# The opening of a fused attention and expert kernel: chunk 0's inverse placed ahead of the weight conversion and alternated with chunk 1's, chunk 2's scans and scores moved to earlier slots

## The chip, the cores and the metric

The kernel runs on one core of a Trainium2 chip. The metric is the device time of one execution in microseconds (us), the median of several runs of the same kernel. One more execution is recorded by the hardware profiler; every row below is from it.

A core has five engines with one instruction queue each, worked off strictly in order: TensorE (PE; its weight loads are shown as PEld), VectorE (DVE), ScalarE (ACT), GpSimd (POOL) and SyncE (SP), which here only issues DMA transfers. They wait for one another through semaphores.

## The reference, cut to what matters

```
# 1. recurrence over t = 0..767 for 4 batches x 8 heads, head size 40; state is 40 x 40
y[:, :, t]  = einsum('bhd,bhde->bhe', r_t, state)
Sa          = einsum('bhde,bhe->bhd', state, a_t)
state       = state * w_t[:, :, None, :] - einsum('bhd,bhe->bhde', Sa, b_t) \
              + einsum('bhd,bhe->bhde', v_t, k_t)
# 2. x = y as 3072 tokens x 320;   x = ((x @ w_a) * (x @ w_b)) @ w_out        (d_ff 1536)
# 3. top-1 of 8 experts: logits = x @ w_gate; e = argmax; g = softmax(logits)[e]
#    out = g * (relu(x @ w1[e]) @ w2[e])
```

The matrices w_a, w_b and w_out arrive as 64-bit floating point numbers and are multiplied as two parts, high and low.

## The kernel before

**Chunks.** The recurrence is cut into 12 chunks of 64 steps. Within a chunk the chain over time becomes matrix products and the inverse of a triangular matrix for each batch and head. What happens for a chunk, with the lines that do it: the decay is scanned on DVE (`scans`, L558 to L563), k and b are scaled by it (`scale_bk`, L601), a is scaled on GpSimd (`scale_a`, L574) and spread into a block matrix `ablk` by ScalarE (`spread_a`, L578). `scores` multiplies the blocks on PE for one batch at a time (L611), ScalarE copies the result to SBUF (L619), GpSimd masks it (L621), and SP sends it to DRAM (`nd`, L628). It comes back as `m` in another layout (L677 or L679). `rows` does the transposes of k and b (L644, L647); `relayout` copies a decay array into a layout `gp` with six DMAs (L660).

**The inverse.** `tinv(c)` inverts the triangles of chunk c on DVE in 31 steps of two instructions each: `tmp = m * xt` (L686), then `xt = xt - tmp` (L692). A step needs the step before it. The widths run from 31 elements up to 136 and down to 16. After the last one the result goes to DRAM and back into the scores' buffer (L703, L707, L708). Then `t21a` transposes it on DVE (L725) and PE multiplies it (L729); the stages of the chunk on PE follow (L800, L806, L840, L855, L871, L895), with output scores copied by ScalarE (L876) and masked by GpSimd (L878).

**Conversion.** Each matrix of 64-bit words is loaded in pieces of 256 columns (`raw`, L972 to L975; a piece of the third kind has two halves). A piece takes four instructions on DVE (L420, L424, L433, L435), some on ScalarE (L422, L430, L432, and L443 for a piece with two halves) and two or three on GpSimd (L438, then L445 or L440). The four DVE instructions are called steps here; pieces are counted from 0. L433 writes a buffer that GpSimd's L445 of two pieces before reads.

**Order.** PE, DVE, ScalarE and GpSimd work in the order in which the program writes their instructions; SP's order follows from it too. `mix(steps, others)` lays two lists into one another evenly. The opening is written out in `phase1`: scans and scores of chunk 0 and 1, the inverses, conversion. Behind it stands a loop over chunks with 24 slots each. Two tables of numbers, `FIRST` for chunk 0 and `STEADY` for the others, say in which slot a piece of work is issued; `dv` and `ot` are lists of DVE and other steps that are due in later slots. In slot i of chunk 0, `conv[i]` conversion steps and `tinv[i]` steps of the next chunk's inverse are issued.

Of the kernel before, what the change touches and what calls it, by code (L numbers as in the profile page):

```python
# [39 lines left out]
def kernel_body(tc, I, out, stage="full", dbg=None):  # L40
    nc = tc.nc
    ctx = ExitStack()
    with ctx:
# [36 lines left out]
        with ExitStack() as moe:  # L80
            with tc.manual_schedule(engines={E.PE, E.DVE, E.Activation, E.Pool}):
                down = None if stage == "up" else MoeDown(tc, I, moe, psA, psM, ident, hT, wo, xs)
                phase1(tc, I, cst, drm, psA, psM, ident, hT, mk_ident, wo, xs, span, tiny, down)
                if stage == "up":
                    return
                experts = Experts(tc, I, moe, psA, psM, ident, xs, out)
                down.run(experts, span, tiny, flag)
# [32 lines left out]
def mix(steps, others):  # L120

    a, b = len(steps), len(others)
    i = j = 0
    while i < a or j < b:
        if j == b or (i < a and (i + 0.5) * b <= (j + 0.5) * a):
            steps[i]()
            i += 1
        else:
            others[j]()
            j += 1  # L130


def phase1(tc, I, cst, drm, psA, psM, ident, hT, mk_ident, wo, xs, span, tiny, down):
# [4 lines left out]
    A = Attention(tc, I, att, mid, cst, drm, psA, ident, dv, ot, span)  # L138
    A.sink, M.pc = M, A.p2

    def run(fs):
        for f in fs:
            f()

    conv = M.weight_steps()
# [6 lines left out]
    sp = A.p2.tile([128, 2 * 256], I32, tag="raw", name="sp0"), A.p2.tile([128, 2 * 256], I32, tag="raw", name="sp1")  # L152
# [32 lines left out]
    tinv = A.tinv(0)  # L185
# [3 lines left out]
    for pr in range(2):  # L189
        A.scale_a(1, pr)  # L190
        A.spread_a(1, pr)
    n0, n1, n2, n3 = FIRST["conv0"]
    run(conv.take(n0))
    for b in range(B):
        A.scores(1, b)
    for b in range(B):
# [2 lines left out]
    uh = [view(M.p2.tile([128, 2, 256], F32, tag="uh", name=f"m1_{h}")) for h in range(2)]  # L199
    xt = M.p2.tile([128, 2, 256], F32, tag="wo", name="xt1", bufs=1)  # L200
    t1 = A.tinv(1, (uh, view(xt)))
    run(conv.take(n1))
    A.relayout(0)
    A.relayout(1)
    mix(tinv, conv.take(n2))
    A.load_w(2)
    for h in range(2):
        A.load_bk(2, h)
    lead = FIRST["lead"]
    mix(t1[:lead], [lambda: A.forward((0, 0))] + conv.take(n3))  # L210
    t1 = t1[lead:]
    over = [A.spans(0, [t[:120, 0:L // 2].bitcast(F32) for t in sp])]
    units, tinv = [], t1
    for c in range(NCH + 1):
# [10 lines left out]
        for i in range(24):  # L225
# [52 lines left out]
            if c2 < NCH:  # L278
                if c == 0:
# [5 lines left out]
                    for k in range(2):  # L285
                        if i == T["over"][k]:
                            if k:
                                sp = [A.p2.tile([128, 2 * 256], I32, tag="raw", name=f"sp{q + 2}") for q in range(2)]
# [55 lines left out]
            if 2 <= c < 10 and i == T["fill"]:  # L344
                k = nz * (c - 2)
# [5 lines left out]
            tinv = tinv[n:]  # L351
            if i == T["inverse"] and c2 < NCH:
                assert not tinv
                tinv = A.tinv(c2)
# [9 lines left out]
    if not down:  # L364
# [19 lines left out]
FIRST = {  # L384
    "order": [
        [("t21a", 0)], [("t21b", 0), ("t21a", 1)],
        [("pu", 0, 0), ("t21b", 1), ("px", 0, 1)],
        [("stage2p", 0, 1)], [("pu", 0, 1)],
        [("stage2v", 0, 1), ("stage2p", 2, 3)], [], [("stage3", 0, 1)], [],
        [], [("stage4", 0, 1)], [("stage2v", 2, 3)], [],  # L390
        [("stage5", 0, 1), ("stage3", 2, 3)], [], [("px", 1, 0)],
        [("stage4", 2, 3)], [], [], [("stage5", 2, 3)], [], [], [], []],
    "conv0": [8, 6, 10, 8], "lead": 16, "early": 13, "extra": [10, 17], "ones": [2, 14],
    "conv": [
# [6 lines left out]
    "load_a": [19, 21], "r00": [2, 3, 4], "r1": [8, 9, 10], "score": [15, 16, 17, 18], "row": [16, 17, 22, 23],  # L401
    "tinv": [4, 4, 4, 4, 4, 4, 4, 4, 4, 4, 4, 2, 0, 0, 0, 0, 0, 0, 0, 0, 0, 0, 0, 0], "relayout": 14, "load_w": 15,
    "span": 18, "scan": [21, 22, 22, 23, 23],
}

# [1428 lines left out]
```

## Time and profile before

| what | value |
|---|---|
| median of 3 runs | 1122.64 us (1122.29 to 1123.97) |
| profiled execution, its time | 1123.74 us |
| profiled execution, its span | 1122.0 us |
| PE busy | 987.2 us, 88% of the span |
| DVE busy | 699.5 us, 62% |
| ACT busy | 592.1 us, 53% |
| POOL busy | 422.8 us, 38% |

The span runs from the first to the last instruction that the profiler saw; the time of that execution lies a little over it. A busy share is a mean over the whole span: it says nothing on which engine the others wait for in a given stretch, for which the rows further down are cut by time.

### The profile page before, as it was taken

Reading aid. Unit: us, or ns where it says so; the run is one execution under the profiler, and the core shown is the slowest. Engines: PE = TensorE matmul, PEld = TensorE weight load, DVE = VectorE, ACT = ScalarE, POOL = GpSimd, SP = SyncE. Lnnn points to the kernel's source line nnn. Section 1 sums busy time; section 2 is a strip of 40 time slices with the busy share of each in tenths; the row PEclk is TensorE's granted clock in tenths of the full one; section 3 lists DMA queues with packets and bytes.
Section 4 is the critical chain, followed back from the end, with each engine's and each line's share of the span. In section 5 each row is a group of like instructions: output and inputs, shape, how many; then the busy total and the mean of one; then the engine's idle time right before and its main releaser. Section 6 shows DMA issues by size and latency. Waiting matters only on the chain.

```text
span 1122.0 us, 27118 instructions
## 1 busy us (share of the span) xinstructions
PE 987.2 (88%) x10402; PEld 948.1 (85%) x10402; DVE 699.5 (62%) x1843; ACT 592.1 (53%) x1373; POOL 422.8 (38%) x469
## 2 busy tenths in 40 slices
PE   4064587999899999999999999999999999999994
PEld 4053587989889899999898999999999898999994
DVE  8889689677787878787866731336667733222230
ACT  5367866666666666666665453333334354444430
POOL 4327645233323323343333113002224466666641
PEclk9656689999999999999999999979999999999997
DMA  8553454476758476675746223825557264444500
GB/s 209 149 159 82 99 135 104 124 144 166 146 153 172 129 168 145 136 157 143 152 130 122 76 75 90 239 68 159 182 177 236 87 220 139 141 146 140 160 17 16
DMA packets 200664, 154.11 MB, mean 137 GB/s; under 512 B 107269, under 2 KB 182630, under 8 KB 200524
## 3 DMA queue, kind: packets, MB, share of 16 engines
q1 hardware_dynamic: 187196, 132.91, 44.8%
q0 software_dynamic: 9808, 15.76, 5.6%
q10 hardware_dynamic: 3520, 3.61, 1.2%
q8 instruction: 84, 1.38, 0.5%
q14 instruction: 56, 0.46, 0.1%
HBM read 103.66 MB, written 44.60 MB: 132 GB/s over the span
## 4 chain that ended last, share of the span: by engine, by line
PE 71%; DVE 10%; DMA 6%; ACT 5%; issue 4%; SPq 2%; POOL 1%; POOLq 0%; DVEq 0%; ACTq 0%
PE pm L1071 23%; PE py L1208 9%; PE u L1497 8%; PE dn L1517 7%; PE s1p L611 4%; PE p L871 3%; PE pp L855 2%; PE py L895 2%; PE px L800 2%; DVE xt L692 1%; PE ta L729 1%; DMA out<-y,ids 1%; DVE tmp L686 1%; PE tb L748 1%; PE px L791 1%
## 5 line engine op out<-in xcount | busy, mean ns | idle before, releaser
L878 POOL TENSOR_SCALAR_AFFINE_SELECT s<-s 64x512 f32<-64x512 f32 x96 | 72.4, 755 | 180.8 <-ACT s L876 176.6
L686 DVE TENSOR_TENSOR tmp<-m,xt 128x126 f32<-128x126 f32 (+22 forms) x372 | 115.1, 310 | 30.5 <-DMA xt<-in_one 19.0
L1083 DVE TENSOR_TENSOR uh<-pm,ua 128x256 f32<-128x256 f32 x144 | 60.4, 419 | 114.5 <-PE pm L1071 67.1
L1071 PE MATMUL pm<-xl,wh 128*128 128x256 f32 x576 | 130.7, 309 | 0.8 <-ACT ua L1074 0.8
L1500 DVE SCALAR_TENSOR_TENSOR hl<-u,hh 128x384 fp32r<-128x384 f32 (+5 forms) x72 | 41.5, 580 | 140.1 <-ACT hh L1499 140.1
L692 DVE TENSOR_TENSOR xt<-xt,tmp 128x126 f32<-128x126 f32 (+22 forms) x372 | 115.3, 310 | 8.6
L1071 PE MATMUL pm<-xh,wl 128*128 128x256 f32 x576 | 117.7, 286 | 0.0
L1071 PE MATMUL pm<-xh,wh 128*128 128x256 f32 x576 | 117.6, 286 | 0.0
L1071 PEld LDWEIGHTS pm<-xl,wh 128*128 128x128 f32 x576 | 90.5, 195 | 3.5 <-ACT ua L1074 1.2
L1208 PE MATMUL py<-wh,hl 128*128 128x328 f32 x288 | 91.3, 317 | 2.0 <-DVE hl L1198 2.0
L1208 PE MATMUL py<-wl,hh 128*128 128x328 f32 x288 | 92.3, 321 | 0.6 <-DVE wl L1179 0.6
L1071 PEld LDWEIGHTS pm<-xh,wh 128*128 128x128 f32 x576 | 91.7, 196 | 0.0
L1071 PEld LDWEIGHTS pm<-xh,wl 128*128 128x128 f32 x576 | 91.4, 195 | 0.0
L1208 PE MATMUL py<-wh,hh 128*128 128x328 f32 x288 | 90.9, 316 | 0.0
L611 PE MATMUL s1p<-ablk,bk 120*128 120x192 f32 (+1 forms) x264 | 53.1, 345 | 41.6 <-ACT ablk L578 30.1
L611 PEld LDWEIGHTS s1p<-ablk,bk 120*128 120x128 f32 x264 | 47.0, 211 | 44.3 <-ACT ablk L578 43.8
L1071 PE MATMUL pm<-xh,w 128*128 128x256 f32 x288 | 82.7, 287 | 0.0
L1071 PE MATMUL pm<-xl,w 128*128 128x256 f32 x288 | 82.6, 287 | 0.0
L1261 POOL DMA_INDIRECT xs<-xr,si x24 | 28.0, 1166 | 137.4 <-DVE acc L1256 89.2
L1074 ACT COPY ua<-pm 128x256 f32<-128x256 f32 x144 | 53.4, 371 | 46.8 <-PE pm L1071 44.3
L1517 PE MATMUL dn<-l,hh 128*128 128x320 f32 (+3 forms) x240 | 74.9, 312 | 0.0
L1517 PE MATMUL dn<-h,hl 128*128 128x320 f32 (+3 forms) x240 | 74.1, 309 | 0.0
(238 smaller groups left out, 2775.4 us busy)
## 6 DMA issues: line engine op xcount, KB each, us to landing
hT<-uh SPq DMA_DIRECT2D x72, 256.0 KB
hf<-hT SPq DMA_DIRECT2D x36, 512.0 KB
r<-in_moe_w SPq DMA_DIRECT2D x8, 1280.0 KB
r<-in_moe_w SPq DMA_DIRECT2D x8, 1024.0 KB
bk<-in_bk SPq DMA_DIRECT2D x22, 360.0 KB
xs<-zt SPq DMA_DIRECT2D x8, 805.0 KB
m<-nd SPq DMA_DIRECT2D x44, 128.0 KB
at<-in_a SPq DMA_DIRECT2D x24, 180.0 KB
```

The source lines that it names most:

```text
L611: nc.tensor.matmul(ps[:2 * C, 3 * g * C:(3 * g + n) * C], self.bk5(c, b, g), self.ablk[b // 2][:, b % 2, g, 0:n, 0:C], start=True, stop=True)
L686: nc.vector.tensor_tensor(box[0], m[2 * s // R][:, s % (R // 2):s % (R // 2) + 1, s + 1:].to_broadcast([128, rows, n]), xt[:, :rows, s:s + ...
L692: nc.vector.tensor_tensor(xt[:, :rows, s + 1:], xt[:, :rows, s + 1:], box[0], op=ALU.subtract)
L871: nc.tensor.matmul(p2[b][:, 3 * g * C:(3 * g + n) * C], self.cur[b]["uv"][:, 128 * g:128 * g + 128], self.rblk[:, b % 2, g, 0:n, 0:C], sta ...
L878: nc.gpsimd.affine_select(out=s2t[q * C:q * C + C], in_=s2t[q * C:q * C + C], pattern=[[0, 8], [1, C]], base=0, channel_multiplier=-1, com ...
L1071: nc.tensor.matmul(p, l, r, start=(i == 0), stop=(i == len(seq) - 1))
L1074: nc.scalar.copy(a, p)
L1083: nc.vector.tensor_tensor(h[:, f % 2], p, a, op=ALU.mult)
L1208: self.nc.tensor.matmul(py, self.pair[i][l][:, k, s], self.W[r][:, first + k, cols], start=(first + k == 0 and n == 0), stop=(first + k == ...
L1497: nc.tensor.matmul(p, l, r, start=(i == 0), stop=(i == len(seq) - 1))
L1500: nc.vector.scalar_tensor_tensor(out=hl, in0=p, scalar=0.0, in1=hh.bitcast(F32), op0=ALU.max, op1=ALU.subtract)
L1517: nc.tensor.matmul(p, l[:, q], r[:, f], start=(f == 0 and i == 0), stop=(f == len(hs) - 1 and i == 2))
```

## The change

It touches the opening and the table for chunk 0. The eight conversion steps that stood ahead of chunk 1's scores, and six behind chunk 1's `rows`, are no longer there; the first 28 instructions of chunk 0's inverse come first on DVE, mixed with 16 conversion steps, and the other 34 are mixed one to one with the first 34 of chunk 1's. Four more of chunk 1's, chunk 0's first stages and four conversion steps follow. The slots' table takes three conversion steps in each of the first twelve slots instead of two, and 24 instructions of chunk 1's inverse in six slots instead of 46 in twelve. Chunk 2's decay limits, scans, scaling, blocks and scores are issued in earlier slots. No instruction is added or taken away; DVE has as many as before.

```diff
-    n0, n1, n2, n3 = FIRST["conv0"]
-    run(conv.take(n0))
     for b in range(B):
         A.scores(1, b)
...
     t1 = A.tinv(1, (uh, view(xt)))
-    run(conv.take(n1))
     A.relayout(0)
     A.relayout(1)
-    mix(tinv, conv.take(n2))
+    n0, n1 = FIRST["conv0"]
+    lead = FIRST["lead"]
+    mix(tinv[:lead], conv.take(n0))
+    k = len(tinv) - lead
+    mix(tinv[lead:], t1[:k])
     A.load_w(2)
     for h in range(2):
         A.load_bk(2, h)
-    lead = FIRST["lead"]
-    mix(t1[:lead], [lambda: A.forward((0, 0))] + conv.take(n3))
-    t1 = t1[lead:]
+    mix(t1[k:k + 4], [lambda: A.forward((0, 0))] + conv.take(n1))
+    t1 = t1[k + 4:]
...
-    "conv0": [8, 6, 10, 8], "lead": 16, "early": 13, "extra": [10, 17], "ones": [2, 14],
+    "conv0": [16, 4], "lead": 28, "early": 13, "extra": [10, 17], "ones": [2, 14],
...
-    "over": [2, 7], "span2": 4, "scan2": 9, "bk": [12, 13], "sa": [12, 13], "sp": [[13, 14, 15], [14, 15, 16]],
+    "over": [2, 7], "span2": 1, "scan2": 3, "bk": [6, 7], "sa": [6, 7], "sp": [[7, 8, 9], [8, 9, 10]],
```

On DVE the order of before has three whole pieces of conversion behind the scaling of chunk 1's k and b. The rows are the third piece's, the start of the fourth, and the start of chunk 0's inverse; `c_f` and `c_s` are a piece's buffers, `raw0_1_0` its words, `m0` and `xt0` belong to chunk 0's inverse.

```order
L420 TENSOR_SCALAR c_f_367<-raw0_1_0_171 128x256
L424 SCALAR_TENSOR_TENSOR c_f_367<-raw0_1_0_171,c_f_367 128x256
L433 TENSOR_SCALAR c_s_368<-c_f_367 128x256
L435 SCALAR_TENSOR_TENSOR c_s_368<-raw0_1_0_171,c_s_368 128x256
L420 TENSOR_SCALAR c_f_382<-raw0_1_1_278 128x256
L424 SCALAR_TENSOR_TENSOR c_f_382<-raw0_1_1_278,c_f_382 128x256
L686 TENSOR_TENSOR tmp0_0_402<-m0_242,xt0_243 128x31
L692 TENSOR_TENSOR xt0_243<-xt0_243,tmp0_0_402 128x31
```

In the new order of DVE the inverse follows the scaling at once, and the fourth piece's first step is row 49, counted from the program's start. The first piece below is from around it, the second from where chunk 0's fifteenth step begins to alternate with chunk 1's first.

```order
L692 TENSOR_TENSOR xt0_243<-xt0_243,tmp0_10_421 128x6x21
L420 TENSOR_SCALAR c_f_429<-raw0_1_1_374 128x256
L686 TENSOR_TENSOR tmp0_11_434<-m0_242,xt0_243 128x120
L692 TENSOR_TENSOR xt0_243<-xt0_243,tmp0_11_434 128x6x20
L424 SCALAR_TENSOR_TENSOR c_f_429<-raw0_1_1_374,c_f_429 128x256
L686 TENSOR_TENSOR tmp0_12_438<-m0_242,xt0_243 128x133
```

```order
L686 TENSOR_TENSOR tmp0_14_448<-m0_242,xt0_243 128x136
L686 TENSOR_TENSOR tmp1_0_450<-m1_0_323,xt1_325 128x31
L692 TENSOR_TENSOR xt0_243<-xt0_243,tmp0_14_448 128x8x17
L692 TENSOR_TENSOR xt1_325<-xt1_325,tmp1_0_450 128x31
L686 TENSOR_TENSOR tmp0_15_454<-m0_242,xt0_243 128x128
L686 TENSOR_TENSOR tmp1_1_456<-m1_0_323,xt1_325 128x30
L692 TENSOR_TENSOR xt0_243<-xt0_243,tmp0_15_454 128x8x16
L692 TENSOR_TENSOR xt1_325<-xt1_325,tmp1_1_456 128x30
```

The fourth piece's first step stood ahead of the inverse; now it stands 34 rows into it, and in the 68 alternating rows there is nothing but the two inverses.

On SP the fourth piece's load stood behind chunk 0's second r and ahead of chunk 1's scores on their way to DRAM.

```order
L588 DMA r0_1_255<-in_r 120x384
L972 DMA raw0_1_1_278<-in_moe_w_b 128x512
L628 DMA nd1_128<-s1_1_0_295 32x8x32 x4
L628 DMA nd1_128<-s1_1_1_312 32x8x32 x4
L680 DMA xt1_351<-in_one 128x512
L677 DMA m1_0_349<-nd1_128 32x512
```

In the new order of SP it stands behind the loads of chunk 1's m and behind both relayouts, whose last rows these are.

```order
L660 DMA gp0_335<-w0_113 64x4x64 x2
L660 DMA gp1_342<-w30_r_124 120x4x64
L660 DMA gp1_342<-w30_r_124 8x4x64
L660 DMA gp1_342<-w30_r_124 112x4x64
L660 DMA gp1_342<-w30_r_124 16x4x64
L660 DMA gp1_342<-w30_r_124 64x4x64 x2
L972 DMA raw0_1_1_374<-in_moe_w_b 128x512
L974 DMA raw0_0_2_400<-in_moe_w_a 64x512
L975 DMA raw0_0_2_400<-in_moe_w_b 64x512
L972 DMA raw256_0_0_426<-in_moe_w_a 128x512
```

The load moved behind eight loads of m and twelve issues of the relayouts.

On GpSimd, behind the masks of chunk 0's first pair of output scores, the new order reads as follows (`s2_0_1` is an output score, `s1_2_0` a score of chunk 2, `at2` chunk 2's a).

```order
L878 AFFINE_SELECT s2_0_1_962<-s2_0_1_962 64x512 x2
L574 TENSOR_TENSOR at2_1_642<-at2_1_642,w2_562 120x384
L438 TENSOR_TENSOR c_f_936<-c_f_936,w30_0_596 64x256
L438 TENSOR_TENSOR c_f_936<-c_f_936,w31_0_597 64x256
L440 TENSOR_TENSOR c_f_936<-c_f_936,c_s_937 128x256
L438 TENSOR_TENSOR c_f_985<-c_f_985,wh00_0_351 128x256
L445 TENSOR_TENSOR wl0_107<-c_f_985,c_s_986 128x256
L621 AFFINE_SELECT s1_2_0_1021<-s1_2_0_1021 64x512 x2
L438 TENSOR_TENSOR c_f_1005<-c_f_1005,wh01_0_376 128x256
L445 TENSOR_TENSOR wl0_107<-c_f_1005,c_s_1006 128x256
```

Before, the first L621 of chunk 2's scores stood further back, behind the masks of the second pair of output scores, the scaling of `at2_1`, a piece with two halves and `xl` (L1050):

```order
L878 AFFINE_SELECT s2_0_3_1106<-s2_0_3_1106 64x512 x2
L574 TENSOR_TENSOR at2_1_654<-at2_1_654,w2_545 120x384
L544 MEMSET d1_91 120x13
L438 TENSOR_TENSOR c_f_1084<-c_f_1084,w30_1_1082 64x256
L438 TENSOR_TENSOR c_f_1084<-c_f_1084,w31_1_1083 64x256
L440 TENSOR_TENSOR c_f_1084<-c_f_1084,c_s_1085 128x256
L1050 TENSOR_TENSOR xl0_1147<-xf0_0_1093,xh0_1146 128x3x128
L621 AFFINE_SELECT s1_2_0_1183<-s1_2_0_1183 64x512
L438 TENSOR_TENSOR c_f_1140<-c_f_1140,wh00_1_1139 128x256
L445 TENSOR_TENSOR wl0_107<-c_f_1140,c_s_1141 128x256
L621 AFFINE_SELECT s1_2_0_1183<-s1_2_0_1183 64x512
L621 AFFINE_SELECT s1_2_1_1251<-s1_2_1_1251 64x512
```

Chunk 2's four masks moved ahead of the second pair's, in between pieces 10 to 13. On ScalarE the blocks of ablk moved as well: the third block for chunk 2's first score stands twelve rows behind L443 of piece 9, and before five rows behind L443 of piece 14.

## Rows read from the trace of the kernel before

**Rows 1.** The page: busy tenths of the span in 40 slices of 28 us.

```profile
PE   4064587999899999999999999999999999999994
DVE  8889689677787878787866731336667733222230
```

**Rows 2.** Windows: stretch, length, busy time and instructions by engine, TensorE clock, DMA.

```profile
31.30:55.60 24.30, 0.00 (x0) 0.00 (x0) 21.15 (x73) 7.09 (x20) 5.86 (x8) 0.55 0.59 156
87.90:111.70 23.80, 9.24 (x97) 8.29 (x97) 21.62 (x38) 16.22 (x45) 19.51 (x23) 0.65 0.37 85
```

**Rows 3.** Timeline of DVE: start, length (both us), engine, line, operation, tiles.

```profile
42.57 0.29 DVE L686 TENSOR_TENSOR tmp<-m,xt 128x126 f32<-128x126 f32 x1
42.90 0.29 DVE L692 TENSOR_TENSOR xt<-xt,tmp 128x126 f32<-128x126 f32 x1
43.10 0.29 DVE L433 TENSOR_SCALAR c_s<-c_f 128x256 int32<-128x256 int32 x1
...
54.98 0.60 DVE L692 TENSOR_TENSOR xt<-xt,tmp 128x16 f32<-128x16 f32 x1
...
55.71 0.19 DVE L692 TENSOR_TENSOR xt<-xt,tmp 128x31 f32<-128x31 f32 x1
55.93 0.19 DVE L686 TENSOR_TENSOR tmp<-m,xt 128x30 f32<-128x30 f32 x1
56.04 0.42 DVE L435 SCALAR_TENSOR_TENSOR c_s<-raw,c_s 128x256 f32<-128x256 uint32 x1
...
62.31 0.89 DVE L725 STREAM_TRANSPOSE t<-s 32x256 f32<-32x256 f32 x2
```

**Rows 4.** Timeline of SP's queue: length is the time of issuing.

```profile
26.07 0.40 SPq L972 DMA_DIRECT2D raw<-in_moe_w_b  x1
...
31.93 3.56 SPq L677 DMA_DIRECT2D m<-nd  x8
...
37.38 5.15 SPq L660 DMA_DIRECT2D gp<-w  x6
42.57 4.46 SPq L660 DMA_DIRECT2D gp<-w_r  x6
```

**Rows 5.** Chain that ended last, cut to the first 260 us: from issue to landing.

```profile
36.11 2.76 DMA raw<-in_moe_w_b
```

**Rows 6.** Timeline of PE; brackets: idle time before, who ended it.

```profile
62.88 0.28 PE L729 MATMUL ta<-t,s 32*32 32x32 f32 x2 [33.07 <-DVE t L725]
...
112.79 2.07 PE L611 MATMUL s1p<-ablk,bk 120*128 120x192 f32 x6 [11.52 <-DVE c_f L420]
```

**Rows 7.** Timeline of ACT.

```profile
87.22 1.06 ACT L876 COPY s<-p 128x512 f32<-128x512 f32 x2
...
109.67 0.83 ACT L443 CAST w<-c_f 64x256 fp32r<-64x256 f32 x2 [1.83 <-POOL c_f L440]
```

**Rows 8.** Timeline of POOL.

```profile
87.86 4.34 POOL L878 TENSOR_SCALAR_AFFINE_SELECT s<-s 64x512 f32<-64x512 f32 x4 [7.41 <-ACT s L876]
...
102.71 3.27 POOL L878 TENSOR_SCALAR_AFFINE_SELECT s<-s 64x512 f32<-64x512 f32 x4
...
107.19 1.65 POOL L438 TENSOR_TENSOR c_f<-c_f,w 64x256 f32<-64x256 f32 x2
...
111.44 1.17 POOL L1050 TENSOR_TENSOR xl<-xf,xh 128x384 fp32r<-128x384 f32 x1 [1.80 <-ACT xh L1049]
...
116.41 0.72 POOL L438 TENSOR_TENSOR c_f<-c_f,wh 128x256 f32<-128x256 f32 x1
...
123.38 0.65 POOL L621 TENSOR_SCALAR_AFFINE_SELECT s<-s 64x512 f32<-64x512 f32 x1
```

**Rows 9.** Timeline of DVE, up to chunk 1's first transposes.

```profile
117.97 0.29 DVE L433 TENSOR_SCALAR c_s<-c_f 128x256 int32<-128x256 int32 x1 [4.75 <-POOL wl L445]
...
123.46 1.41 DVE L433 TENSOR_SCALAR c_s<-c_f 128x256 int32<-128x256 int32 x1 [4.08 <-POOL wl L445]
...
131.11 0.89 DVE L725 STREAM_TRANSPOSE t<-s 32x256 f32<-32x256 f32 x2
```

More of the change, by code (lines that the diff above doesn't have):

```diff
@@ L399 @@
         2, 1, 2, 1, 2, 1, 2, 1, 2, 2, 1, 1],
[1 row of a table removed]
-    "load_a": [19, 21], "r00": [2, 3, 4], "r1": [8, 9, 10], "score": [15, 16, 17, 18], "row": [16, 17, 22, 23],
-    "tinv": [4, 4, 4, 4, 4, 4, 4, 4, 4, 4, 4, 2, 0, 0, 0, 0, 0, 0, 0, 0, 0, 0, 0, 0], "relayout": 14, "load_w": 15,
[1 row of a table added]
+    "load_a": [19, 21], "r00": [2, 3, 4], "r1": [8, 9, 10], "score": [9, 10, 11, 12], "row": [12, 17, 22, 23],
+    "tinv": [4, 4, 4, 4, 4, 4, 0, 0, 0, 0, 0, 0, 0, 0, 0, 0, 0, 0, 0, 0, 0, 0, 0, 0], "relayout": 14, "load_w": 15,
     "span": 18, "scan": [21, 22, 22, 23, 23],
```

2 rows, old and new, of the table FIRST are left out of this document.

## The prediction

> **What bounds the kernel now.** I read the busy tenths first. VectorE (DVE) is at 8 or 9 in most of the first seven slices of 28 us while TensorE (PE) stands between 0 and 7; from the eighth slice on PE stands at 8 or 9 [rows 1]. So the opening belongs to DVE and what feeds it, the rest to PE, and time gained or lost in the opening shifts all that follows. The order says where the change ends: from the 226th row on, 18 rows ahead of chunk 1's transposes (L725), DVE's orders read the same, PE's from chunk 1's first L729. So the forecast is one question: when does DVE begin those transposes? Before it is 131.11 us [rows 9]; a shift there I carry to the end unchanged, since DVE and PE have little idle time behind it [rows 1].
>
> Next the windows and DVE's timeline. From 31.30 to 55.60 DVE works through chunk 0's inverse with ten conversion steps between, 73 rows in 24.30 us, 0.333 us a row, and PE does nothing [rows 2]. Single starts tell what a step costs. A product 126 elements wide starts at 42.57, the subtraction that needs it at 42.90: 0.33. The next instruction, which needs neither, starts 0.20 later [rows 3]. Narrow ones (30 or 31 wide): 0.22 to a dependent one, 0.11 to an independent one [rows 3]. So a step that doesn't need the result just before it starts a third to a half sooner; this is what alternation can give.
>
> Last subtraction 54.98, its end 0.60 later, hence 55.58 [rows 3]; the inverse goes out through SyncE's queue (SP) to DRAM and back, and DVE's transposes start at 62.31 [rows 3], PE's first L729 at 62.88 after 33.07 us of idling [rows 6]. That tail is 62.31 - 55.58 = 6.7 us.
>
> **Part 1: the conversions behind the scores, and a load that moves with them.** No conversion step stands ahead of the inverse any more. This removes a load's early place too: the fourth piece's words (raw0_1_1, L972) were sent at 26.07, ahead of chunk 1's scores' way to DRAM [rows 4]. In the new order of SP they stand behind the 8 loads of chunk 1's m (L677) and behind all 12 issues of the two relayouts (L660). Those cost SP: the m loads end at 31.93 + 3.56 = 35.49; the relayouts take 5.15 + 4.46 = 9.61 [rows 4]. One issue of 0.40 leaves ahead of them [rows 4], two other pieces that stood between no longer do, so the last relayout is issued at 35.49 - 0.40 + 9.61 = 44.7. A load of such words landed 2.76 after its issue [rows 5]: 47.5. (If the scores come up to 2 us earlier, since ScalarE and DVE have no conversion in front of them, 45.5; that is the lower bound.)
>
> DVE needs that piece in its 49th row, the 35th after the inverse starts. Even if the inverse started only at the old 31.3, the 34 rows at 0.333 are done by 42.6. So DVE waits, everything on it queued behind, until about 47.5: a wait of at least 5 us that wasn't there.
>
> **Part 2: alternation.** Behind the wait stand ten rows of mixed steps, at the mean of 0.33 and 0.20: 2.7 us, hence 50.2. Then 68 rows alternate chunk 0's last 34 steps with chunk 1's first 34. Their mean width, counted from the order, is 96; between 0.11 at 30 and 0.20 at 126 that is 0.17 a row, 11.7 us: chunk 0's inverse ends at 61.9. With dependent starts throughout (0.22 and 0.33, so 0.295) it would be 20.1. I take 0.17, since the row of an independent successor is the nearest.
>
> 61.9 - 55.6 = **+6.3 us** for everything that waits for chunk 0's inverse. The work that DVE has then done is about the same as before at 62 (it has 18 of chunk 1's steps more, 15 of the conversion's fewer). With the tail of 6.7 us PE starts at 62.88 + 6.3 = 69.2. In this tail DVE's new order has only 8 rows: little is left to cover the round trip with.
>
> **Part 3: chunk 2's scans and scores earlier.** Their instructions are the same in number; they shift on ScalarE and GpSimd, among them ablk's blocks (L578) and GpSimd's masks (L621). From PE's start, the chain to the first output score copies of chunk 0 (L876) keeps its instructions: 87.22 [rows 7] + 6.3 = 93.5. GpSimd masks them from 94.1 (87.86 before) for 4.34 [rows 8], then, in its order, a scaling of chunk 2's a (0.72 for 256 columns, so about 1.1 for its 384), and two products and a sum for piece 9, which took 2.5 from 107.19 until L443 was let go at 109.67 [rows 7, 8]: 102.0. ScalarE's L443 waits for that sum, as it did before at 109.67 with 1.83 of idling [rows 7]; now the blocks of ablk for chunk 2's first score stand behind it, after 18 instructions at 16.22 / 45 = 0.36 [rows 2] L443's own 0.83, and two DMA issues at 0.40 or somewhat more [rows 4], taken at 1.0: 102.0 + 0.8 + 6.5 + 1.0 = 110.3. So the first score of chunk 2 starts on PE at about 111, against 112.79 before [rows 6]: placed 45 rows earlier, it gains no more than 2 us. PE has nearly the same rows from there to the last of the four scores (6 matmuls of L840 for 6 of L644), so the last mask comes as far behind as before, 123.38 - 112.79 = 10.6 [rows 6, 8]: at 121.6.
>
> What stands behind that last mask on GpSimd changes most. Before: two pieces, 4 instructions of 0.72. Now: the mask's own 0.65, piece 13 (2 x 0.72 = 1.5), the masks of chunk 0's second pair (4.34), piece 14 (2.4), the round over ScalarE to xl (1.80 idle, 1.17 of work), and pieces 15 to 18 (4 x 1.5) [rows 8]. Sum 0.65 + 1.5 + 4.3 + 2.4 + 1.8 + 1.2 + 6.0 = 17.9: GpSimd is through at 121.6 + 17.9 = 139.5. DVE's L433 can't write its buffer before GpSimd has done L445 of two pieces back: twice before it waited for that, 4.75 and 4.08 us [rows 9]. So its last two conversion steps start at 139.5 and take about 1.2 (an estimate between the 2 x 0.29 of an undisturbed L433 and the 2 x 1.41 of a slow one [rows 9]): the transposes stand at 140.7, against 131.11: **+9.6 us**.
>
> The profiled execution took 1123.74; 1123.74 + 9.6 = 1133.3. It lies 1.1 over the median of the runs, so the median to come is 1132.2, said as **1132**. Bounds of this case: the load 2 us sooner and the second pair's masks at their shorter 3.27 [rows 8] give +6.5, i.e. 1129; two waits more of the length of 1.8 on GpSimd's way give 1136.
>
> **A rule weighed against the trace.** The row pair shows 0.33 to a dependent step and 0.20 to an independent one [rows 3]. The Trainium skill, "VectorE: DVE Perf Modes", section "The DRAIN you can't avoid", has the next operation start only when the pipe of eight stages is empty; by that alone alternation would give nothing and the 68 rows would cost 20.1. The same page's section "Two Vector instructions with no wait between them" says that one that isn't held starts earlier, which agrees with the 0.20. The first reading is the third rival.
>
> **The rivals.**
> *Faster.* If chunk 2's scores really come early, GpSimd doesn't wait for them and doesn't hold DVE: the two waits of 4.75 and 4.08 [rows 9] go, 8.8 us, against the 6.3: 1122.6 + 6.3 - 8.8 = 1120; without part 1's wait it would be some 5 better. For it: GpSimd's work from 102.0 to the end of piece 15 is only 18 us (pieces 10 to 13 and 15 at 1.5, four masks at 0.65, the second pair's 4.3, piece 14's 2.4, xl's 1.2), so without waits it is there at 120, just when DVE, 6.3 late, comes to need it. It decides by GpSimd's waiting in that stretch: what it waits there comes off the 8.8, and above 2.5 us in all nothing is won. I find more than that at the first mask alone, which stands only 1.5 us of work behind the sum that releases L443, while ScalarE and PE need some 11 from L443 to that score. 13 in 100.
>
> *Only the delay.* The stretch from the copies to the transposes takes as long as before, 131.11 - 87.22 = 43.9, since what the early scores win on ScalarE they lose on GpSimd: +6.3, so 1129. For it: DVE was idle for 8.8 us there, and can run ahead. 22 in 100.
>
> *Each operation waits for the one before it to drain.* Then 8.4 more in part 2: 1132 + 8.4 = 1140. Against: the 0.20 and the 0.11 [rows 3]. 5 in 100; 2 more for other ways above 1136.
>
> *No change.* DVE's work up to the transposes is the same, and its waits only change their names: the wait for the load takes the place of those for GpSimd, within 2.2 us. For it: 4.75 + 4.08 is not far from 6.3 plus the tail's idling. 10 in 100.
>
> **How the numbers follow.** My forecast, 1129 to 1136 with 1132 the likeliest, has 48 in 100. A measurement tells about 0.2%, 2.2 us, from no change. Faster holds 0.13, same 0.10, slower 0.48 + 0.22 + 0.07 = 0.77. The range from 1121 to 1139 takes in forecast, delay alone and no change, and leaves out most of the faster case and the drained one.
>
> **What would show it.** In the changed kernel's trace: a wait of DVE at L420 for raw from in_moe_w_b, ending near 47; rows of 0.17 in the alternating stretch; PE's first L729 near 69; an L443 on ScalarE that ends a wait for GpSimd near 102; chunk 2's last mask near 122; chunk 1's transposes near 141. I am wrong if DVE's 49th row finds its words there, if GpSimd runs without waits from 100 to 130, or if PE's steady part takes back what the opening lost.

## The result and the profile after

The changed kernel takes 1135.93 us (median of 4 runs, 1134.41 to 1136.44) against 1122.52 for the kernel before, measured with it: ratio 1.0133, interval 1.0115 to 1.0151 (the plain quotient of the two medians is 1.0119, near the interval's lower end). It is slower, by a little over one per cent; the forecast range, 1129 to 1136, just holds the time, 4 us above its likeliest value. The profiled execution took 1136.14 us, its span 1134.3.

The page's busy tenths, to be held against [rows 1]: PE first reaches 9 in the ninth slice and no longer in the eighth, and DVE's second slice falls from 8 to 5.

```profile
PE   4042568899999989999999999999999899999994
DVE  6568489686979778796878651335666842222230
```

SP's queue in the changed kernel (start, time of issuing) answers to [rows 4]. The fourth piece's load goes out at 46.06, behind the relayouts, where before it went out at 26.07; the last line is chunk 0's inverse on its way to DRAM.

```profile
32.62 3.57 SPq L677 DMA_DIRECT2D m<-nd  x8
36.29 4.71 SPq L660 DMA_DIRECT2D gp<-w  x6
41.11 4.91 SPq L660 DMA_DIRECT2D gp<-w_r  x6
46.06 0.61 SPq L972 DMA_DIRECT2D raw<-in_moe_w_b  x1
...
64.50 2.65 SPq L703 DMA_DIRECT2D td<-xt  x4
```

DVE's timeline in the changed kernel answers to [rows 3, 9]. The wait of 11.26 us at L420 is the one forecast; the 7.70 at L558, the first scan step of chunk 2, was not. The rows marked x2 show the alternation: two instructions each, the next row 0.33 later, so some 0.17 an instruction. The last wait for GpSimd ahead of the transposes ends at 139.49; from there DVE works through 9.0 us of rows of its own without waiting.

```profile
37.15 0.78 DVE L692 TENSOR_TENSOR xt<-xt,tmp 128x126 f32<-128x126 f32 x1
49.18 0.29 DVE L420 TENSOR_SCALAR c_f<-raw 128x256 int32<-128x256 int32 x1 [11.26 <-DMA raw<-in_moe_w_b]
...
52.32 0.89 DVE L686 TENSOR_TENSOR tmp<-m,xt 128x136 f32<-128x136 f32 x2
53.15 0.40 DVE L692 TENSOR_TENSOR xt<-xt,tmp 128x136 f32<-128x136 f32 x2
53.48 0.39 DVE L686 TENSOR_TENSOR tmp<-m,xt 128x128 f32<-128x128 f32 x2
...
64.63 0.29 DVE L686 TENSOR_TENSOR tmp<-m,xt 128x126 f32<-128x126 f32 x1
...
69.58 0.90 DVE L725 STREAM_TRANSPOSE t<-s 32x256 f32<-32x256 f32 x2 [2.98 <-DMA s<-td]
...
83.90 0.65 DVE L558 TENSOR_SCALAR w<-w 120x768 f32<-120x768 f32 x1 [7.70 <-ACT junk L537]
...
123.66 0.29 DVE L433 TENSOR_SCALAR c_s<-c_f 128x256 int32<-128x256 int32 x1 [9.20 <-POOL wl L445]
...
139.49 0.29 DVE L433 TENSOR_SCALAR c_s<-c_f 128x256 int32<-128x256 int32 x1 [3.40 <-POOL wl L445]
...
147.36 0.75 DVE L433 TENSOR_SCALAR c_s<-c_f 128x256 int32<-128x256 int32 x1
...
148.48 0.89 DVE L725 STREAM_TRANSPOSE t<-s 32x256 f32<-32x256 f32 x2
```

PE's timeline answers to [rows 6]: the first L729 at 70.16, then a wait of 5.32 at L840 for DVE's rows (L850), which stand behind L558 there, and chunk 2's first score at 114.84 after 18.55 us of idling for its blocks.

```profile
70.16 0.28 PE L729 MATMUL ta<-t,s 32*32 32x32 f32 x2 [40.21 <-DVE t L725]
...
90.69 0.89 PE L840 MATMUL pv<-ident,vn 128*120 128x128 f32 x3 [5.32 <-DVE tp L850]
...
114.84 2.07 PE L611 MATMUL s1p<-ablk,bk 120*128 120x192 f32 x6 [18.55 <-ACT ablk L578]
```

ScalarE, answering to [rows 7]: chunk 2's decay limits (L537), whose last row ends at 83.87, just ahead of DVE's L558, and which stand behind L736, which waited for PE's first L729; the output score copies at 98.72, the first block at 99.80, L443 after 6.06 us of waiting for GpSimd, the third block with the next at 114.19.

```profile
71.62 0.78 ACT L736 ACTIVATE pt<-ta 32x256 f32<-32x256 f32 x2 [4.67 <-PE ta L729]
...
83.68 0.19 ACT L537 ACTIVATION_READ_ACCUMULATOR junk<-w,wlim 120x1 f32 x1
...
98.72 1.06 ACT L876 COPY s<-p 128x512 f32<-128x512 f32 x2
99.80 0.62 ACT L578 ACTIVATE ablk<-at,bd 120x384 f32<-120x384 f32 x1
106.48 0.83 ACT L443 CAST w<-c_f 64x256 fp32r<-64x256 f32 x2 [6.06 <-POOL c_f L440]
...
114.19 1.10 ACT L578 ACTIVATE ablk<-at,bd 120x384 f32<-120x384 f32 x2
```

GpSimd, answering to [rows 8]: three waits for ScalarE between 106 and 122, the last mask of chunk 2 at 126.57, the last L445 ahead of the transposes at 145.11.

```profile
111.48 0.72 POOL L438 TENSOR_TENSOR c_f<-c_f,wh 128x256 f32<-128x256 f32 x1 [5.04 <-ACT wh L432]
...
117.66 0.66 POOL L621 TENSOR_SCALAR_AFFINE_SELECT s<-s 64x512 f32<-64x512 f32 x1 [4.65 <-ACT s L619]
121.48 0.65 POOL L621 TENSOR_SCALAR_AFFINE_SELECT s<-s 64x512 f32<-64x512 f32 x1 [3.16 <-ACT s L619]
...
126.57 0.65 POOL L621 TENSOR_SCALAR_AFFINE_SELECT s<-s 64x512 f32<-64x512 f32 x1
...
145.11 0.72 POOL L445 TENSOR_TENSOR wl<-c_f,c_s 128x256 fp32r<-128x256 f32 x1
```

### The profile page after: what moved, and what is told of

It reads as the page before. It is cut to its first block, busy times and chain, and to the rows that moved or that the text cites. A ratio compares the mean times of both kernels' runs of the same rounds, so it can differ in the third digit from the quotient of the medians.

```text
span 1134.3 us, 27119 instructions
## 1 busy us (share of the span) xinstructions
PE 982.0 (87%) x10402; PEld 943.4 (83%) x10402; DVE 690.7 (61%) x1843; ACT 592.1 (52%) x1373; POOL 422.3 (37%) x469
## 4 chain that ended last, share of the span: by engine, by line
PE 67%; DVE 12%; ACT 6%; DMA 5%; issue 5%; POOL 3%; SPq 1%; ACTq 0%; POOLq 0%; DVEq 0%
PE pm L1071 23%; PE py L1208 9%; PE u L1497 6%; PE dn L1517 6%; PE s1p L611 4%; PE p L871 3%; PE pp L855 2%; PE py L895 2%; DVE xt L692 2%; DMA out<-y,ids 2%; PE px L800 2%; DVE tmp L686 1%; PE ta L729 1%; PE kbp L644 1%; PE tb L748 1%
## 5 line engine op out<-in xcount | busy, mean ns | idle before, releaser
L686 DVE TENSOR_TENSOR tmp<-m,xt 128x126 f32<-128x126 f32 (+22 forms) x372 | 110.1, 300 | 31.1 <-DMA xt<-in_one 17.8
L1208 PE MATMUL py<-wh,hl 128*128 128x328 f32 x288 | 91.1, 316 | 2.0 <-DVE hl L1198 2.0
L1208 PE MATMUL py<-wl,hh 128*128 128x328 f32 x288 | 92.1, 320 | 0.6 <-DVE wl L1179 0.6
L1208 PE MATMUL py<-wh,hh 128*128 128x328 f32 x288 | 90.7, 315 | 0.0
L611 PEld LDWEIGHTS s1p<-ablk,bk 120*128 120x128 f32 x264 | 46.7, 210 | 51.6 <-ACT ablk L578 51.1
L1074 ACT COPY ua<-pm 128x256 f32<-128x256 f32 x144 | 53.5, 371 | 44.5 <-PE pm L1071 42.5
L729 PE MATMUL ta<-t,s 32*32 32x32 f32 x768 | 22.6, 202 | 60.5 <-DVE t L725 56.8
```

Of the source, the lines that this page charges most:

```text
L611: nc.tensor.matmul(ps[:2 * C, 3 * g * C:(3 * g + n) * C], self.bk5(c, b, g), self.ablk[b // 2][:, b % 2, g, 0:n, 0:C], start=True, stop=True)
L686: nc.vector.tensor_tensor(box[0], m[2 * s // R][:, s % (R // 2):s % (R // 2) + 1, s + 1:].to_broadcast([128, rows, n]), xt[:, :rows, s:s + ...
L1074: nc.scalar.copy(a, p)
L1208: self.nc.tensor.matmul(py, self.pair[i][l][:, k, s], self.W[r][:, first + k, cols], start=(first + k == 0 and n == 0), stop=(first + k == ...
```

## The experiments

My theory: the change loses by places in queues, first the load behind the relayouts, then the early scores, whose blocks and masks hold conversion. The rivals: the early scores set the pace whatever the load does; or the order of DVE's work as such (inverse first, conversion pushed back) costs the time. Single executions of the kernel before spread from 1117 to 1128 us beside these runs, so ratios to it are compared. The ratio on record differs from the plain quotient of the medians by up to 0.0015; differences as small as that are not read here. The table puts four marks (starts, us) beside the ratio; the marks come from one execution of each kernel, the ratio from all.

| kernel | ratio (interval) | PE's first L729 | first L876 | chunk 2's first score | chunk 1's first L729 |
|---|---|---|---|---|---|
| before | 1 | 62.88 | 87.22 | 112.79 | 131.68 |
| changed | 1.0133 (1.0115 to 1.0151) | 70.16 | 98.72 | 114.84 | 149.06 |
| early load | 1.0069 (1.0050 to 1.0089) | 59.63 | 91.12 | 107.19 | 141.89 |
| old slots | 1.0095 (1.0073 to 1.0118) | 68.14 | 92.61 | 123.63 | 143.87 |
| old opening, early slots | 1.0008 (0.9992 to 1.0024) | 63.20 | 90.30 | 101.86 | 136.24 |
| early load, old slots | 1.0030 (1.0017 to 1.0043) | 59.16 | 86.11 | 118.06 | 137.67 |
| the same, no alternation | 1.0058 (1.0041 to 1.0075) | 64.62 | 88.94 | 119.97 | 139.59 |
| early load, limits earlier | 1.0025 (1.0011 to 1.0039) | 59.17 | 85.96 | 102.39 | 136.62 |
| conversion beside the inverse | 1.0022 (1.0003 to 1.0041) | 61.53 | 90.00 | 115.16 | 134.38 |
| relayouts behind | 1.0065 (1.0046 to 1.0084) | 58.74 | 87.27 | 103.33 | 138.18 |
| the former, four pieces ahead | 0.9978 (0.9958 to 0.9997) | 62.03 | 85.00 | 110.55 | 131.58 |
| change, queues mended | 1.0012 (0.9995 to 1.0029) | 58.97 | 82.67 | 99.23 | 135.18 |
| the same, blocks ahead of L443 | 0.9973 (0.9958 to 0.9988) | 58.25 | 81.99 | 84.97 | 128.44 |
| before with two mends | 0.9935 (0.9912 to 0.9959) | 61.30 | 84.27 | 103.98 | 124.16 |

("The former" is conversion beside the inverse.) The ratio goes, by and large, with the last column and not with the first: nine kernels start PE's work on chunk 0 earlier than before, and only three of them are faster.

**Early load.**

```diff
-        self.ahead = lambda: [load(j) for j in range(3)]
+        self.ahead = lambda: [load(j) for j in range(4)]
```

> The changed kernel, with the fourth piece's words loaded together with the first three (ahead of chunk 0's scores), all else as changed. Theory A (the load's wait costs what it lasts): the wait of 11.26 us at DVE's L420 is gone, chunk 0's inverse ends near 53 instead of 64.5, PE's first L729 stands near 59 instead of 70.2, and the time falls by 9 to 11 us, to about 1126. Theory B (the early scores set the pace on ScalarE and GpSimd whatever chunk 0's inverse does): the wait goes, PE starts near 59, but chunk 1's transposes come less than 5 us earlier than 148.5 and the time stays above 1131.

The wait at the fourth piece's L420 is gone, chunk 0's inverse goes out at 53.64, PE starts at 59.63, as theory A said; 10.5 us there. The ratio falls from 1.0133 to 1.0069, some 7 us (6 by the medians), less than the 9 to 11 expected. Behind PE's start a new wait for words has come in, for the seventh piece, and the wait at L558 is still there:

```profile
68.48 0.29 DVE L420 TENSOR_SCALAR c_f<-raw 128x256 int32<-128x256 int32 x1 [4.96 <-DMA raw<-in_moe_w_a]
...
76.30 0.65 DVE L558 TENSOR_SCALAR w<-w 120x768 f32<-120x768 f32 x1 [5.66 <-ACT junk L537]
```

**Old slots for chunk 2, the changed opening.**

```diff
-    "over": [2, 7], "span2": 1, "scan2": 3, "bk": [6, 7], "sa": [6, 7], "sp": [[7, 8, 9], [8, 9, 10]],
+    "over": [2, 7], "span2": 4, "scan2": 9, "bk": [12, 13], "sa": [12, 13], "sp": [[13, 14, 15], [14, 15, 16]],
...
-    "load_a": [19, 21], "r00": [2, 3, 4], "r1": [8, 9, 10], "score": [9, 10, 11, 12], "row": [12, 17, 22, 23],
+    "load_a": [19, 21], "r00": [2, 3, 4], "r1": [8, 9, 10], "score": [15, 16, 17, 18], "row": [16, 17, 22, 23],
```

> The changed opening, with chunk 2's limits, scans, scaling, blocks and scores back in the slots of before. Theory A (part delay, part early scores): PE's first L729 stays at 70 and the wait of 11 us at L420 stays; the wait of 7.70 at DVE's L558 and the longer road from chunk 0's output score copies to chunk 1's transposes (49.8 us, 43.9 before) go back to before's; chunk 1's transposes near 138 to 139, time about 1129. Theory B (early scores cost nothing, the delay is all): time within 2 us of the changed kernel, 1134 or more.

Between the two: 1.0095, where A said 1129 (1.006); its interval touches the changed kernel's. The wait at L420 stays (9.40 us), the wait of 7.70 at L558 is gone, but the other sign of A failed: the road from the first L876 to chunk 1's first L729 (last column less second) stays long, 51.3 us against 50.3 in the changed kernel and 44.5 before. So the early slots alone don't make this road longer than before.

**Old opening, early slots** (edit on the kernel before).

```diff
-    "over": [2, 7], "span2": 4, "scan2": 9, "bk": [12, 13], "sa": [12, 13], "sp": [[13, 14, 15], [14, 15, 16]],
+    "over": [2, 7], "span2": 1, "scan2": 3, "bk": [6, 7], "sa": [6, 7], "sp": [[7, 8, 9], [8, 9, 10]],
...
-    "load_a": [19, 21], "r00": [2, 3, 4], "r1": [8, 9, 10], "score": [15, 16, 17, 18], "row": [16, 17, 22, 23],
+    "load_a": [19, 21], "r00": [2, 3, 4], "r1": [8, 9, 10], "score": [9, 10, 11, 12], "row": [12, 17, 22, 23],
```

> The opening of before with chunk 2's limits, scans, scaling, blocks and scores in the changed kernel's early slots; conversion and inverse steps per slot as before. Theory A: no wait at L420, PE's first L729 near 63, but L558 waits for ScalarE's limits and GpSimd's masks wait for the scores: chunk 1's transposes 6 to 10 us later than 131, time 1128 to 1132. Theory B (early scores are a gain that the late inverse hid): chunk 1's transposes earlier than 131 and a time below 1120.

Neither: no difference (1.0008). L558 waits 5.89 us and chunk 1's first L729 comes 4.6 us late, yet nearly all of it comes back by the end. The road from the copies is 45.9 us, 1.5 more than before. Chunk 2's first score comes at 101.86, 11 us earlier than before, and DVE's waits for GpSimd don't go by it: 3.04, 5.42, 1.42 and 3.41 ahead of the transposes. So the early slots alone explain little of the loss, and win nothing either.

**Early load and old slots.**

> The changed opening with the fourth piece loaded early and chunk 2's work in the slots of before: what is left of the change is the inverse ahead of conversion and the alternation. Theory A: chunk 0's inverse ends near 53, two to three us before the 55.6 of the kernel before, PE's first L729 near 60, and chunk 1's transposes come as much earlier: 1119 to 1120.5. Theory B (work is only moved about, DVE has the same to do until chunk 1's transposes): 1122 to 1124.

Theory A failed here, and the time, 1125.29, lies a little above B's range as well. PE starts at 59.16, 3.7 us earlier than in the kernel before, and chunk 1's transposes still come 6 us late. DVE again waits for words at L420, and longer than before for GpSimd's pieces:

```profile
68.44 0.29 DVE L420 TENSOR_SCALAR c_f<-raw 128x256 int32<-128x256 int32 x1 [5.38 <-DMA raw<-in_moe_w_a]
...
74.03 0.46 DVE L420 TENSOR_SCALAR c_f<-raw 128x256 int32<-128x256 int32 x1 [3.16 <-DMA raw<-in_moe_w_b]
...
93.82 0.29 DVE L433 TENSOR_SCALAR c_s<-c_f 128x256 int32<-128x256 int32 x1 [3.65 <-POOL c_f L440]
```

The words are now behind the round trip of the earlier inverse: on SP the seventh piece's load is issued at 61.73, after the last load of chunk 0's inverse at 59.79, where the changed kernel issues it at 50.05.

**The same without alternation.**

```diff
-    mix(tinv[lead:], t1[:k])
+    run(tinv[lead:])
+    run(t1[:k])
```

> As the run with the early load and chunk 2's slots of before (1125.3 us), but the last 34 instructions of chunk 0's inverse stand alone, and chunk 1's 34 behind them, in the time of the round trip through DRAM. Theory A (alternation delays the inverse that PE waits for): 34 dependent instructions take 34 x 0.295 = 10.0 us instead of 12.3, PE's first L729 stands near 57 instead of 59.2, the 3 us of waiting ahead of DVE's first L725 vanish, but DVE needs 8 us more in all; since chunk 1's transposes are held by conversion and not by PE's start, they stay within 2 us of 137 and so does the time, 1123 to 1127. Theory B (alternation is what the change is worth): DVE loses 8 us, time 1131 or more.

Neither as written. Chunk 0's 34 instructions alone take 10.4 us and go out at 52.14, 1.3 us earlier than alternated; but chunk 1's 34 stand ahead of the transposes on DVE, outlast the round trip, and PE starts at 64.62 and not at 57. Alternation is worth 1.0058 - 1.0030, some 3 us, in this surrounding (2 by the medians; the two intervals just overlap).

**Early load, chunk 2's limits one slot earlier** (with the early load).

```diff
-    "over": [2, 7], "span2": 1, "scan2": 3, "bk": [6, 7], "sa": [6, 7], "sp": [[7, 8, 9], [8, 9, 10]],
+    "over": [2, 7], "span2": 0, "scan2": 3, "bk": [6, 7], "sa": [6, 7], "sp": [[7, 8, 9], [8, 9, 10]],
```

> The changed kernel with the early load (1129.8 us), and chunk 2's limits issued one slot earlier, so that ScalarE has them sooner than DVE's first scan step of chunk 2 (L558) asks for them. Theory A (that scan's wait of 5.66 us is paid in full, since the transfer of PE's work, L850, stands behind it): the wait falls to 2 us or less and the time by 3 to 4 us, to about 1126. Theory B (the road over GpSimd and ScalarE is the longer one): the wait falls and the time stays within 1.5 us.

Theory A: no wait at L558, and the ratio falls from 1.0069 to 1.0025, some 5 us. It comes out no worse than with the old slots (1.0030): what the early slots cost on top of the load is, in this surrounding, the scan's wait and not the place of the scores.

**Conversion beside the inverse** (edit against the changed kernel).

```diff
-    mix(tinv[lead:], t1[:k])
+    mix(tinv[lead:], conv.take(n1))
...
-    mix(t1[k:k + 4], [lambda: A.forward((0, 0))] + conv.take(n1))
+    mix(t1[:16], [lambda: A.forward((0, 0))] + conv.take(n2))
```

with `conv0` [16, 8, 8], the early load, the slots' tables of before, and both `relayout` calls behind the first `mix`.

> Chunk 0's inverse ahead of all conversion as in the change, but its last 34 instructions are mixed with 8 conversion steps and not with chunk 1's inverse, whose steps go back to the slots of before, as do conversion's and chunk 2's; the fourth piece is loaded early and the relayouts are issued behind the first 28 instructions. Six pieces of conversion are then done when chunk 0's inverse ends, where the change has four. Theory A (what is left of the loss, 4 us, is conversion that lags): chunk 0's inverse ends near 51, chunk 1's transposes come by 128 to 132, time 1118 to 1122.5. Theory B (the order of DVE's work up to the transposes is indifferent): 1124 to 1126, as with the early load and the old slots.

Chunk 1's L729 at 134.38, 3 us sooner than with alternation (137.67), but 2.7 later than before. The time, 1124.84, is in B's range, DVE's transposes (133.80) are past A's window, and the ratio's interval, 1.0003 to 1.0041, reaches down to A's range of times: B is the likelier, not more. The road from the copies is back at 44.4 us, as before, against 51.6 with the early load and old slots; but PE also starts 2.4 us later than there. A wait of 5.42 us at L420 for raw is in this trace too (68.90).

**The changed kernel, relayouts behind the first 28 instructions.**

```diff
-    A.relayout(0)
-    A.relayout(1)
...
     mix(tinv[:lead], conv.take(n0))
+    A.relayout(0)
+    A.relayout(1)
```

> The changed kernel with one thing moved: both relayouts are issued behind the first 28 instructions of chunk 0's inverse and not ahead of them, so that the fourth piece's load and the next ones go out ahead of their twelve issues. Theory A (the wait at L420 comes from the place in SP's queue): the load is issued near 35, the wait falls from 11.3 to 1 or 2 us, PE's first L729 stands near 61, time 1128 to 1131, as with the early load. Theory B (the load is late for another reason, a buffer or the memory): the wait stays above 5 us and the time above 1133.

Theory A, by a second way: the load is issued at 34.94, DVE's L420 runs at 37.92 with no wait, and the ratio is 1.0065, the early load's 1.0069.

**Four pieces ahead**, on the kernel with conversion beside the inverse.

```diff
-            for d in range(3 if self.early or self.extra else 2):
+            for d in range(4 if self.early else 3 if self.extra else 2):
```

with `load_w(2)` and `load_bk(2, h)` moved to right behind the relayouts, from behind the second `mix`:

```diff
     A.relayout(1)
+    A.load_w(2)
+    for h in range(2):
+        A.load_bk(2, h)
```

> As the run with conversion beside chunk 0's inverse (ratio 1.0022), and while the first buffers last four pieces are sent ahead and not three, with chunk 2's w and k sent before the last part of chunk 0's inverse. The wait of 5.42 us at DVE's L420 (words sent behind the round trip of the inverse) should go. Theory A (what keeps that kernel from gaining is this wait for words): chunk 1's transposes near 129 to 131 instead of 134, ratio 0.996 to 0.999. Theory B (ScalarE and GpSimd set the pace of conversion): ratio stays at 1.001 to 1.003.

The wait at L420 near 69 is gone, the ratio 0.9978 (0.9958 to 0.9997) is A's. DVE's transposes start at 131.01, at the end of the window that I gave, and chunk 1's L729 (131.58) is where it was before. So the traces don't show where these 2 us are won; the two profiled executions have the same span, 1122.0.

**The change, queues mended:** relayouts behind, four pieces ahead, chunk 2's w and k early, limits a slot earlier, on the changed kernel; the edits are those of the early load, the earlier limits, the relayouts behind and the four pieces ahead:

```diff
-        self.ahead = lambda: [load(j) for j in range(3)]
+        self.ahead = lambda: [load(j) for j in range(4)]
...
-            for d in range(3 if self.early or self.extra else 2):
+            for d in range(4 if self.early else 3 if self.extra else 2):
```

> The whole change with three places in the queues mended: relayouts behind the first 28 instructions of chunk 0's inverse, four pieces sent ahead in the opening with chunk 2's w and k before the alternating part, chunk 2's limits one slot earlier. No wait at L420 near 49 and near 69, none at L558. Theory A (the change loses by its queue places alone): first L729 near 59, chunk 1's transposes near 131, ratio 0.997 to 1.000. Theory B (the two pieces of conversion that alternation pushed back cost 2 to 3 us by themselves): ratio 1.002 or more, with DVE waiting for GpSimd's L445 for some 18 us between 95 and 130.

PE starts at 58.97, but chunk 1's L729 stands at 135.18: 1.0012, no difference from before, between the two theories in time. No wait for words is left near 49 or 69; 2.81 us of the wait at L558 are. DVE's waits for GpSimd are those of theory B, 4.80, 9.15, 0.62, 1.42 and 3.40, 19.4 us.

**The same, blocks ahead of L443.**

```diff
-    "over": [2, 7], "span2": 0, "scan2": 3, "bk": [6, 7], "sa": [6, 7], "sp": [[7, 8, 9], [8, 9, 10]],
+    "over": [2, 7], "span2": 0, "scan2": 3, "bk": [6, 7], "sa": [6, 6], "sp": [[7, 7, 7], [7, 8, 8]],
```

> As the mended kernel, and all three blocks for chunk 2's first score stand on ScalarE ahead of L443 of piece 9, with both scalings of chunk 2's a ahead of the masks of the output scores on GpSimd. Theory A (that L443, waiting 6 us for GpSimd, holds the blocks, PE's first score of chunk 2, GpSimd's masks and so DVE's conversion): PE's idling ahead of the first score falls from 16 to 8 us or less, DVE's wait of 9.3 us for L445 to 4 or less, time 3 to 5 us below the mended kernel's. Theory B (conversion on ScalarE and GpSimd is the longer road): the score comes earlier, the time stays within 1.5 us of the mended kernel's.

Theory A. The kernel without it, PE and DVE, first:

```profile
99.23 2.07 PE L611 MATMUL s1p<-ablk,bk 120*128 120x192 f32 x6 [16.68 <-ACT ablk L578]
```

```profile
108.06 0.29 DVE L433 TENSOR_SCALAR c_s<-c_f 128x256 int32<-128x256 int32 x1 [9.15 <-POOL wl L445]
```

and with it:

```profile
84.97 2.07 PE L611 MATMUL s1p<-ablk,bk 120*128 120x192 f32 x6 [3.12 <-ACT ablk L578]
```

```profile
103.04 0.29 DVE L433 TENSOR_SCALAR c_s<-c_f 128x256 int32<-128x256 int32 x1 [4.71 <-POOL wl L445]
```

The score comes 14 us earlier, this wait of DVE is halved (4.71 where A had said 4 or less; the one of 4.80 ahead of it stays), and the ratio falls from 1.0012 to 0.9973, some 4 us. The edit moves the other blocks and the second scaling of a on GpSimd along with the three; they weren't tried apart.

**The kernel before with the two mends that don't need the change:** four pieces ahead (both of its edits, as in the run with the queues mended), and the blocks earlier in its own slots.

```diff
-    "over": [2, 7], "span2": 4, "scan2": 9, "bk": [12, 13], "sa": [12, 13], "sp": [[13, 14, 15], [14, 15, 16]],
+    "over": [2, 7], "span2": 4, "scan2": 9, "bk": [12, 13], "sa": [12, 12], "sp": [[13, 13, 13], [13, 14, 14]],
```

> The kernel before with the two queue mends that the best kernel (ratio 0.9973) carries and that are independent of the change: four pieces sent ahead in the opening, and the blocks for chunk 2's first score ahead of the next L443 on ScalarE. Theory A (the best kernel's gain comes from these mends): ratio 0.996 to 0.999, chunk 1's transposes near 128. Theory B (it needs the order of the change, with the inverse first and the scores early): ratio 0.999 to 1.001, transposes within 1 us of 131.

Theory A, and more than it said: 0.9935, 1113.75 us, the fastest of all. Its DVE waits for L445 are 2.16 and 1.42 where [rows 9] have 4.75 and 4.08:

```profile
112.36 0.72 DVE L433 TENSOR_SCALAR c_s<-c_f 128x256 int32<-128x256 int32 x1 [2.16 <-POOL wl L445]
115.94 1.42 DVE L433 TENSOR_SCALAR c_s<-c_f 128x256 int32<-128x256 int32 x1 [1.42 <-POOL wl L445]
```

PE's first L729 moves by 1.6 us, the first copies by 3.0, chunk 1's L729 by 7.5; by where they arise I put the first 3 us to the pieces' loads and the other 4.5 to the blocks, but this isn't shown: the two mends weren't run apart.

## Why the prediction was right, and where its steps were off

**The load behind the relayouts: right.** Forecast: sent near 44.7, landed at 47.5, a wait of at least 5 us. Measured: sent at 46.06, DVE resumes at 49.18 after 11.26. Two separate edits take the wait away and some 7 us of the time with it.

**Alternation: right in its price.** The 68 rows take 64.63 - 52.32 = 12.3 us, 0.181 a row; forecast 0.17 and 11.7. The run without alternation gives 10.4 / 34 = 0.306 for dependent starts; forecast 0.295. The rival by which each operation waits for the pipe to empty is out: it would have had 20.1. The Trainium skill's page "VectorE: DVE Perf Modes" says in its section "The DRAIN you can't avoid" that a next operation that is not held starts earlier, and points to its section "Two Vector instructions with no wait between them" for it. The trace agrees: behind a row of 0.29 us one that doesn't need it starts after 0.20 [rows 3]; the flat reading, by which each waits for an empty pipe, doesn't fit it.

**"+6.3 for everything that waits for chunk 0's inverse": mis-sized.** The inverse went out 8.9 us late (64.50 against 55.61), mostly since DVE had the words at 49.18 and not at 47.5; PE's first L729 came 7.3 late, since the round trip was shorter (5.1 us to DVE's transposes, 6.7 before).

**"The chain to the first output score copies keeps its instructions": this step failed.** It keeps them, but a wait came in: from L729 to L876 98.72 - 70.16 = 28.6 us, against 24.3. I moved chunk 2's first scan step forward in the sum without asking what it waits for. It needs the decay limits, which ScalarE has on its list behind work that itself waits for PE's start, and DVE's L850, for which PE waits, stands behind it. One slot for the limits gave back 5 us, in the kernel with the early load.

**Part 3: its waits are there, but the early slots aren't their price.** L443 waited for GpSimd, the third block behind it, the score at 114.84 (forecast 111 with PE's start a microsecond and the copies five earlier), the last mask 126.57 (121.6), GpSimd through at 145.8 (139.5), the transposes at 148.48 (140.7). The tail behind the last mask was 19.3 us, forecast 17.9. That L443 holds the blocks was shown by moving them: 4 us. Two things were wrong in it. The last join isn't GpSimd's end: DVE's last wait for it was over at 139.49, then DVE had 9.0 us of rows of its own, and its last L433 started at 147.36, 1.5 us after GpSimd was through. And the longer road from the copies to the transposes (3.3 us in the sum, 47.2 against 43.9; measured 49.8) can't be put down to the early slots: with the old slots it is as long, and in the old opening the early slots add 1.5 us. By the table (last column less second) it is 50.3 to 52.5 us in every kernel with the change's order of inverses and conversion, alternating or not, except the one with the blocks moved (46.5), and 39.9 to 46.6 in the others. That points to the conversion steps that this order pushes back, which no run moved alone.

**"A shift there I carry to the end unchanged": failed the other way.** The reason given, little idle time of DVE and PE [rows 1], holds for PE at most: DVE stands at 7 tenths or less from the 21st slice on, in more than half of these slices at 3 or less. 17.4 us at the transposes are still 17.5 at chunk 2's first L729 (212.43 against 194.91), but 14.5 at the third part's first L1208 (756.2 against 741.7) and 12.3 in the span (13.4 by the medians). The 5 us go in small pieces, some 3 ahead of the third part and 2 in it; what makes them good stays open. The two errors, 7.8 too few at the transposes and 5 too many after, partly cancel: that 1132 came as near to 1136 as it did is luck.

**"The work that DVE has then done is about the same": right in count, wrong in kind.** Conversion pieces pass over three engines with two buffers between; chunk 1's steps need DVE alone and nobody waits for them before the transposes. With the load mended and the old slots, PE began 3.7 us early and the transposes came 6 late, with waits for words and for GpSimd in between.

**The rivals.** *Faster* was out by the sign that the prediction gave for it, GpSimd's waiting: 5.04, 4.65 and 3.16 us between 106 and 122, where 2.5 were allowed. It named the right prize, DVE's two waits for L445, but early scores alone don't win it, as the old opening with early slots shows; it was reached in part (2.16 and 1.42 are left of 4.75 and 4.08) with the blocks ahead of L443 and more pieces sent ahead, on the kernel before best of all. *Only the delay* is out as well: the road behind the copies took 49.8 us and not 43.9.

**What the loss was made of.** Mend by mend the ratio went from 1.0133 to 1.0069 (the load), 1.0025 (the limits), 1.0012 (the queues) and 0.9973 (the blocks). So these places in queues are worth the whole loss and more. Whether the new order of DVE's work costs something by itself stays open: two of the mends gain in the order of before as well, which gets to 0.9935 where the mended change gets to 0.9973 (with more mends, so the difference isn't one edit's). For the gain the order of the change isn't needed.

## What to carry to other kernels

When code that issues loads is moved, print the queue's order and look for what now stands ahead of each load: here a load that ended up behind twelve issues of the relayouts kept DVE waiting for 11.26 us, almost as long as the whole alternating stretch took. Starting PE's work earlier gained nothing here while the next join waited for a pipeline over three engines; follow the time of that join instead. An instruction that waits on another engine should have nothing behind it that a third engine needs: moving the blocks, and the scaling before them, ahead of one cast was worth 4 us.

## What the runs showed that I had not expected

Filling a round trip can be too much of a good thing: 34 instructions of chunk 1 between the last subtraction and the transposes cost PE 5.5 us of its start (64.62 against 59.16), though DVE idled there for 2.9 us otherwise. And the kernel's time follows the start of chunk 1's first L729 over fourteen kernels, from 7.5 us early to 17.4 late: by the ratios the end is shifted by between 0.8 us more and 3.7 less than that start.
